# One predicated copy per score bank, a new switch table for the planner, and plain steps placed one by one

## The chip, the cores and the metric

The kernel runs on one core of one Trainium2 chip. The metric is the device time of one execution in microseconds (us); lower is better. Five engines work side by side, each on a queue of its own that it takes in order: TensorE (PE in the profile, with its weight loads listed apart as PEld), VectorE (DVE), ScalarE (ACT), GpSimd (POOL) and SyncE (SP, which starts the transfers). They wait for one another only through semaphores.

## The reference

```python
def _attn_ref(q, k, v):                      # q, k, v: (8, 8, 576, 64) float32
    scores = scale * np.matmul(q, k.transpose(0, 1, 3, 2))
    bias = slopes[:, None, None] * (-np.abs(rel))[None, :, :]
    mask = (rel >= 0) & (rel < 128)          # each row sees itself and the 127 before it
    scores = np.where(mask, scores + bias[None], -1e9)
    attn = softmax(scores)                   # max, exp, sum + 1e-9, divide
    return np.matmul(attn, v)

def _moe_ref(x, w_gate, w_val, w_out):       # x: (4608, 512), d_ff = 1536
    gate = sigmoid(x @ w_gate)
    return (gate * (x @ w_val)) @ w_out
```

The attention output, heads side by side, is the x of the gated feed-forward part.

## The kernel before

The attention is cut into 32 units, one for a batch and a pair of heads (576 rows of two heads, nine blocks of 128 rows). In a unit, `scores` works on four blocks at a time (a stage): TensorE writes the scores of 128 query rows against the keys that they can see into a bank of PSUM; a predicated copy on VectorE folds the two triangles that the window leaves into one square of 128 by 128; a custom VectorE instruction (line 394) adds the bias and takes the row minimum; ScalarE takes the exponential (397). For three blocks together, `probabilities` adds 1e-9 and inverts the sums on VectorE (412, 414), scales the rows (417 on ScalarE or 418 on VectorE, as the planner chooses), turns the three squares on TensorE (422), copies them out of PSUM (183 or 184) and masks them on GpSimd (433). When nine blocks are done, `values` multiplies with v (483), and copies and one addition (495) bring the result out; it is stored to DRAM as `xs`.

The first eight units ("whole") use matmuls of 64 by 128 for the scores and one copy of 128 partitions for a bank (line 386). The 24 units behind them ("fine") use the array as four squares of 64 by 64: `quarters` writes only the visible quarters, score matmuls are line 369, and the fold is two copies of 64 partitions for each bank (line 382), one for each half of the rows.

TensorE's other work during the attention is `gates1`, the gate and value products of four of the twelve chunks of d_ff for the first 3072 tokens: six tiles of 512 tokens, each with eight sums of twelve full-array matmuls of 512 columns (line 540, 576 in all). These are the plain steps. They take x of one tile at a time from a buffer `x1` that is used again for the next tile, through two banks. In the kernel before, `project` adds them to the plan in threes (one chunk of x in three products of high and low parts). Behind the last plain step come `gates2` (line 622) and `results` (line 731), with full-array matmuls alone.

Nothing of this order stands in the code as such. Every step is added to a `Graph` with an engine, an estimated cost, its reads and writes, and a wish time `want`. `order` then picks, again and again, the step that could start earliest by these costs (ties by `want`; plain steps have the latest), and `play` writes the instructions in order of the planned start. On the chip each engine keeps that order: a step that isn't ready holds everything behind it on its engine. The field `mode` says how TensorE's array is cut for a step; a step of another mode than the one ahead is put off by a fixed time:

```python
            if o.eng == "PE" and o.mode != mode:
                mode = o.mode
                o.start += SWITCH / 2
```

Until 30 us, `play` also fills TensorE's planned holes with dummy matmuls (line 243).

Of the kernel before, what the change touches and what calls it, by code (L numbers as in the profile page):

```python
# [12 lines left out]
ALU = mybir.AluOpType  # L13
PSUM = bass.MemoryType.PSUM

P = 128
B, H, S, D = 8, 8, 576, 64
# [24 lines left out]
RPACE = 6.5  # L42
SLACK = 0.5
W0, WSTEP = 25.0, 1.0
SWITCH = 0.2
WARM = 30.0
YIELD = {"DVE": 0.1, "POOL": 0.0}
NRAW = 2
# [11 lines left out]
class Graph:  # L60
# [38 lines left out]
    def order(self):  # L99
        free = dict.fromkeys(self.LAT, 0.0)  # L100
        free["PE"] = 1.5
        wait = []
        port = moved = 0.0
        mode = 0
        for o in self.ops:
            if not o.left:
                wait.append(o)
        n = 0
        while n < len(self.ops):
            best = None  # L110
            for o in wait:
                least = min(way[1] for way in o.ways)
                for k, way in enumerate(o.ways):
                    e, cost, lat, shared, emit = way
                    s = max(free[e], o.ready, port if shared else 0.0)
                    key = (s + cost - least + (YIELD[e] if k else 0.0), o.want, o.seq)
                    if best is None or key < best[0]:
                        best = key, o, way, s
            key, o, (o.eng, o.cost, o.lat, shared, o.emit), o.start = best
            if o.eng == "PE" and o.mode != mode:  # L120
                mode = o.mode
                o.start += SWITCH / 2
            if o.eng == "PE" and o.start < WARM:
                gap = (o.start - free["PE"] - 0.2) // (0.25 if free["PE"] > 5.0 else 0.45)
                if gap > 0:
                    self.fill.append((free["PE"] + 0.01, int(gap)))
            wait.remove(o)
            if o.size:
                moved = max(moved, o.start + 1.7) + o.size
                o.lat = moved + 0.4 - o.start  # L130
            free[o.eng] = o.start + o.cost
            if shared:
                port = o.start + o.cost
            n += 1
            for i in o.outs:
                d = self.ops[i]
                same = o.eng == "PE" and d.eng == "PE"
                d.ready = max(d.ready, o.start + (o.cost if same else o.lat + d.slack))
                d.left -= 1
                if not d.left:  # L140
                    wait.append(d)
        return sorted(self.ops, key=lambda o: (o.start, o.seq))
# [10 lines left out]
def dve_cost(n, psum=False, two=False):  # L153
    return 0.07 + n * (0.00104 if psum or two else 0.00053)
# [7 lines left out]
def attention_gated_ffn(ctx: ExitStack, tc: tile.TileContext, qd, kd, vd, wg, wv, wo, out):  # L162
    nc = tc.nc
    ctx.enter_context(tc.manual_schedule())
    g = Graph()
# [38 lines left out]
    rel = ring[:, 0:3 * P].rearrange("p (a q) -> p a q", a=3)  # L204
    nc.gpsimd.iota(rel[:, 0], [[-1, P]], base=0, channel_multiplier=1, allow_small_or_imprecise_dtypes=True)
    before = att.tile([P, 2, P], I32, name="before")
    swap = att.tile([P, 2, D], I32, name="swap")
# [15 lines left out]
    nc.vector.tensor_scalar_mul(r0[:, 4], r0[:, 1], 0.5)  # L223
    for p in range(1, NPAIR):
        nc.vector.tensor_scalar_mul(relm[p], r0, 4.0 ** -p)
    for a in range(2):
        nc.gpsimd.tensor_scalar(swap[0:D, a], rel[0:D, 0, 0:D], 0.0, None, op0=ALU.is_ge)
        nc.gpsimd.tensor_copy(swap[D:P, a], rel[D:P, 1, D:P])

    xs = [dram.tile([KC, P, S], F32, name=f"xs{b}") for b in range(B)]  # L230
    hs = [[dram.tile([NFC // 2, P, HALVES[b // 2]], F32, name=f"hs{k}_{b}") for b in range(2 * NT2)] for k in range(2)]
# [4 lines left out]
    mm = [ps_m.tile([P, NB], F32, name=f"mm{i}") for i in range(8)]  # L236
    sp = [t.rearrange("p (a q) -> p a q", a=2) for t in mm[2:6]]
    tp, avp, avo = mm[6].rearrange("p (a q) -> p a q", a=4), mm[7], mm[5]
    TP, TAIL, AVP, AVO = ("mm", 6), ("mm", 6, TRI), ("mm", 7), ("mm", 5)

    def warm(n):
# [12 lines left out]
    w1 = lambda kind, part_: T(moe, "w1", [P, 2, 2, FC1, DM], F32R, tag="wA")[:, "gv".index(kind), part_]  # L254
# [89 lines left out]
    def scores(blks):  # L344

        u0, i0 = blks[0]
        want = u0.when(i0)
        slack = 0.0 if u0.n < HEAD else SLACK
        spot = [(k % 2, k // 2) for k in range(len(blks))]
        fine = u0.n >= HEAD  # L350
# [20 lines left out]

        used = sorted({place(r, a) // 2 for r, a in spot}, key=lambda b: [place(r, a) // 2 for r, a in spot].index(b))
        of_bank = {b: [(u, i, place(r, a) % 2) for (u, i), (r, a) in zip(blks, spot) if place(r, a) // 2 == b] for b in used}
        cost = 0.163 * len(blks) + 0.1 if fine else sum(max(0.216 if i == 0 else 0.432 for u, i, a in on) for on in of_bank.values())
        g.add("PE", cost, quarters if fine else whole,
              [("qr", u.l, i) for u, i in blks] + [("kr", u.l, j) for u, i in blks for j in (i - 1, i) if j >= 0],
              [("mm", 2 + b) for b in used], want, slack=slack, release=max(u.rel(i) for u, i in blks), mode=1)
        for b in used:
            if fine:
                for h in range(2):  # L380
                    col, to, of = slice(h * D, h * D + D), D + h * D, 0 if h else 3 * D
                    g.add("DVE", dve_cost(2 * D, psum=True), lambda b=b, col=col, to=to, of=of: nc.vector.copy_predicated(  # L382
                        sp[b][col, :, to:to + D], swap[col], sp[b][col, :, of:of + D]), ["before"], [("mm", 2 + b)], want)
            elif a := [a for u, i, a in of_bank[b] if i]:
                a0, a1 = a[0], a[-1] + 1
                g.add("DVE", dve_cost((a1 - a0) * P, psum=True), lambda b=b, a0=a0, a1=a1: nc.vector.copy_predicated(  # L386
                    sp[b][:, a0:a1, P:], before[:, a0:a1], sp[b][:, a0:a1, 0:P]), ["before"], [("mm", 2 + b)], want)
# [18 lines left out]
    def probabilities(u, i0):  # L406
        m, _, st, pb, kst, kpb = three_of(u, i0)
        want = u.when(i0 + TRI)
        slack = 0.0 if u.n < HEAD else SLACK
        n, kb = TRI, ("both", m % NBOTH)  # L410
        both = lambda: T(att, f"both{m % NBOTH}", [P, TRI, P], F32)
        g.add("DVE", 0.07, lambda: nc.vector.tensor_scalar_add(st()[:, 6:9], st()[:, 3:6], 1.0e-9),
              [(kst, 3 + e) for e in range(n)], [(kst, 6)], want)
        g.add("DVE", 0.09, lambda: nc.vector.reciprocal(st()[:, 6:9], st()[:, 6:9]), [], [(kst, 6)], want)  # L414
        for e in range(n):
            args = lambda e=e: (pb()[:, e], pb()[:, e], st()[:, 6 + e:7 + e])
            g.add("ACT", 0.3, lambda args=args: nc.scalar.mul(*args()), [(kst, 6)], [(kpb, e)], want,  # L417
                  ways=[("DVE", 0.16, True, lambda args=args: nc.vector.tensor_scalar_mul(*args()))])  # L418

        def transpose():  # L420
            for e in range(n):
                nc.tensor.transpose(tp[:, e], pb()[:, e], ident)  # L422

        g.add("PE", 0.11 * n + 0.1, transpose, [(kpb, e) for e in range(n)], [TP], want, slack=slack)
        copy(lambda: both(), lambda: tp[:, 0:n], n * P, [TP], [kb], want, psum=True)
        for own in range(2):
            step, cmp, mult = ([1, P], ALU.is_ge, -1) if own else ([-1, P], ALU.is_gt, 1)

            def spread(own=own, step=step, cmp=cmp, mult=mult):
                f0 = 2 * i0 + own
                nc.gpsimd.affine_select(pt(u)[:, f0:f0 + 2 * n - 1:2, :], both(), [[0, n], step], cmp, 0.0,  # L433
                                        base=0, channel_multiplier=mult)

            g.add("POOL", 0.13 + 0.12 * n, spread, [kb], [("pt", u.n % NPT, i0 + e, own) for e in range(n)], want)
# [3 lines left out]
    def values(u):  # L440
        want = u.when(NBLK + 1)
        slack = 0.0 if u.n < HEAD else SLACK
        spots = ((0, NB, lambda: avp), (NB, S, lambda: tp[:, TRI, 0:S - NB]))
        runs = []
        for t0, t1, to in spots:
            todo = [[], []]
            for e in range(2):
                for c in range(NBLK):

                    a, b = max(c * P, e * S + t0), min((c + 2) * P, NBLK * P, e * S + t1)  # L450
# [11 lines left out]
        fine = u.n >= HEAD  # L462
# [12 lines left out]
        def quarters():  # L475
            seen = pt(u).rearrange("p s t -> p (s t)")
            begun = set()
            for _, e, jj, t0, t1 in quarter:
# [6 lines left out]
                begun.add((k, e))  # L485

        need = [("pt", u.n % NPT, i, own) for i in range(NBLK) for own in range(2)]
        g.add("PE", 1.5 if fine else 1.81 + 0.15, quarters if fine else matmuls, need + [("vr", u.l)],
              [AVP, TAIL] + [AVO] * fine, want, slack=slack, mode=1 if fine else 2)
        xt = lambda: T(att, f"xt{u.s}", [P, S], F32)  # L490
        for (t0, t1, to), key in zip(spots, (AVP, TAIL)):
            copy(lambda t0=t0, t1=t1: xt()[:, t0:t1], lambda t0=t0, t1=t1, to=to: to()[:, 0:t1 - t0], t1 - t0, [key], [("xt", u.s, t0)],
                 want, psum=True)
# [26 lines left out]
    def gates1(t0, n):  # L520
        F = FIRST
        xr = lambda: xrow()[:, :, 0:n]
        a = t0
        while t0 and a < t0 + n:
            b = a // S
            e = min((b + 1) * S, t0 + n)
# [3 lines left out]
            a = e  # L530
# [4 lines left out]
        def project(kind, i):  # L535
            s = bank()
            for c in range(KC):
                def three(c=c):
                    for k, (wi, x) in enumerate(((0, 0), (1, 0), (0, 1))):
                        nc.tensor.matmul(mm[s][:, 0:n], w1(kind, wi)[:, i, c * P:(c + 1) * P], x1(x)[:, c, 0:n],  # L540
                                         start=(k == 0 and c == 0), stop=(k == 2 and c == KC - 1))
                g.add("PE", 3 * (n / 2400 + 0.0177), three, [("w1", kind, wi, i) for wi in range(2)] + [("xhi", c), ("xlo", c)],
                      [("mm", s)], 1.0e6)
            return s

        for i0 in range(0, FC1, GRP):
            grp = range(i0, min(FC1, i0 + GRP))
            for i in grp:
                s = project("g", i)
# [384 lines left out]
```

## Time and profile before

| what | value |
|---|---|
| three runs | 1003.98, 1005.03, 1005.67 us; median 1005.03 |
| the profiled execution | 1005.5 us, of which the span of the profile is 1003.7 |
| mean granted TensorE clock | 0.996 |
| PE busy | 986.3 us (98%), 6498 instructions |
| DVE busy | 837.0 us (83%), 2104 instructions |
| ACT busy | 526.9 us (52%) |
| POOL busy | 123.6 us (12%) |
| first score matmul of the fine units | 59.05 us |
| last matmul of the attention | 320.57 us |
| last plain step, first matmul of line 622 | 335.6 us |

The busy share of PE is a weak sign, since matmuls overlap: a plain step shows about 410 ns, while they follow each other every 230 ns. The waits ahead of the weight loads (PEld) show more of what TensorE lacked. "Releaser" is the instruction whose semaphore ended a wait, and "issue" is time in which nothing that the profile shows was waited for.

### The profile page before, as it was taken

The page shows a single profiled execution, that of the slowest core. Times are in us where ns is not written, and L with a number is a line of the kernel's source. Part 1 is how long each engine was busy: PE and PEld are TensorE (multiplying, and loading weights), DVE is VectorE, ACT ScalarE, POOL GpSimd, SP SyncE. Part 2 cuts the span into 40 slices and gives each one's busy share as a digit, 9 for nine tenths or more (in the row PEclk, how much of TensorE's full clock was granted, in tenths as well). Part 3 has the DMA queues.
Part 4 walks back from the last instruction along what each step waited for, and adds up shares of the span by engine and source line. Part 5 has one row for each costly group of instructions (what it writes and reads, how often), then busy time and mean ns, then how long its engine had stood idle before and what let it go on. Part 6 is the DMA issues. An engine that isn't in the chain of part 4 may idle for free.

```text
span 1003.7 us, 18582 instructions
## 1 busy us (share of the span) xinstructions
PE 986.3 (98%) x6498; PEld 836.5 (83%) x6498; DVE 837.0 (83%) x2104; ACT 526.9 (52%) x1365; POOL 123.6 (12%) x225
## 2 busy tenths in 40 slices
PE   9899899999999999999999999999999999999998
PEld 8667677677777888788888999999998888889998
DVE  8998888988986999977943897599899988888883
ACT  6998887677875554534623454354356232312230
POOL 2333334123322001000000000000010000000000
PEclk9999899999999999999999999999999999999999
DMA  8765767564734454467421344144635635252601
GB/s 290 259 225 182 228 225 274 177 219 169 243 108 152 160 168 155 151 247 237 145 92 63 112 141 147 48 152 126 226 102 189 218 115 182 71 168 89 189 16 63
DMA packets 82845, 163.74 MB, mean 163 GB/s; under 512 B 8256, under 2 KB 34752, under 8 KB 82752
## 3 DMA queue, kind: packets, MB, share of 16 engines
q1 hardware_dynamic: 82752, 162.56, 48.6%
q8 instruction: 51, 0.84, 0.3%
q14 instruction: 42, 0.34, 0.1%
HBM read 112.20 MB, written 50.33 MB: 162 GB/s over the span
## 4 chain that ended last, share of the span: by engine, by line
PE 75%; DVE 18%; ACT 4%; issue 2%; DMA 1%; POOL 0%; SPq 0%; ACTq 0%; DVEq 0%; POOLq 0%
PE mm L622 34%; PE mm L731 26%; PE mm L540 7%; DVE mm L382 3%; PE mm L369 2%; DVE pb L394 2%; ACT pb L397 2%; PE mm L483 2%; DVE work L280 2%; PE mm L422 2%; DVE pb L418 1%; DVE x L192 1%; DVE ring L556 1%; DVE mm L386 1%; PE mm L243 1%
## 5 line engine op out<-in xcount | busy, mean ns | idle before, releaser
L540 PE MATMUL mm<-x,w 128*128 128x512 f32 x576 | 157.3, 409 | 1.7 <-DVE x L192 1.0
L622 PE MATMUL mm<-cxA,w2s 128*128 128x384 f32 (+1 forms) x684 | 145.0, 361 | 0.0
L622 PE MATMUL mm<-cxB,w2s 128*128 128x384 f32 (+1 forms) x684 | 143.9, 361 | 0.0
L397 ACT ACTIVATE pb<-pb,st 128x128 f32<-128x128 f32 x288 | 112.9, 395 | 44.6 <-DVE st L394 43.8
L622 PEld LDWEIGHTS mm<-cxA,w2s 128*128 128x128 f32 x684 | 123.8, 188 | 12.8
L622 PEld LDWEIGHTS mm<-cxB,w2s 128*128 128x128 f32 x684 | 123.6, 188 | 12.7
L433 POOL TENSOR_SCALAR_AFFINE_SELECT pt<-both 128x384 f32<-128x384 f32 x192 | 100.9, 549 | 203.2 <-ACT both L183 183.5
L540 PEld LDWEIGHTS mm<-x,w 128*128 128x128 f32 x576 | 101.1, 189 | 29.4 <-issue 7.6
L183 ACT COPY ring<-mm 128x512 f32<-128x512 f32 (+1 forms) x143 | 75.4, 534 | 78.4 <-PE mm L622 77.1
L731 PE MATMUL mm<-cxA,wos 128*128 128x512 f32 (+1 forms) x540 | 113.6, 368 | 0.0
L731 PE MATMUL mm<-cxB,wos 128*128 128x512 f32 (+1 forms) x540 | 113.3, 367 | 0.0
L731 PEld LDWEIGHTS mm<-cxB,wos 128*128 128x128 f32 x540 | 98.4, 188 | 12.6
L731 PEld LDWEIGHTS mm<-cxA,wos 128*128 128x128 f32 x540 | 98.4, 188 | 12.6
L633 ACT ACTIVATE sg<-mm 128x512 f32<-128x512 f32 (+1 forms) x96 | 52.2, 545 | 107.4 <-PE mm L622 59.8
L629 DVE TENSOR_TENSOR mm<-mm,ring 128x512 f32<-128x512 f32 (+1 forms) x96 | 60.2, 629 | 49.9 <-PE mm L622 49.6
L280 DVE SCALAR_TENSOR_TENSOR work<-work 128x512 int32<-128x512 int32 x104 | 70.9, 694 | 0.5
L394 DVE CUSTOM_DVE_ANT_0 pb<-mm,relm 128x128 f32<-128x128 f32 x288 | 68.6, 285 | 1.7
L191 POOL TENSOR_TENSOR work<-work 128x256 f32<-128x256 f32 x19 | 16.6, 878 | 399.7 <-ACT ring L183 210.1
L422 PE MATMUL mm<-ident,pb 128*128 128x128 f32 x288 | 52.7, 288 | 8.9 <-ACT both L183 4.5
L382 DVE COPY_PREDICATED mm<-swap,mm 64x128 f32<-64x128 int32 x216 | 56.1, 294 | 5.4 <-PE mm L369 1.6
L417 ACT ACTIVATE pb<-pb,st 128x128 f32<-128x128 f32 x163 | 56.3, 396 | 7.1 <-DVE st L414 6.5
L743 ACT ACTIVATE ring<-mm 128x512 f32<-128x512 f32 (+1 forms) x40 | 22.3, 556 | 69.5 <-PE mm L731 69.5
(110 smaller groups left out, 1594.1 us busy)
## 6 DMA issues: line engine op xcount, KB each, us to landing
hs<-ring SPq DMA_DIRECT2D x72, 256.0 KB, 2.1
kr<-in_k_dram SPq DMA_DIRECT2D x31, 576.0 KB, 5.0
work<-in_moe_w_gate_dram SPq DMA_DIRECT2D x20, 512.0 KB, 3.7
work<-in_moe_w_val_dram SPq DMA_DIRECT2D x20, 512.0 KB, 4.5
qr<-in_q_dram SPq DMA_DIRECT2D x31, 320.0 KB, 5.4
vr<-in_v_dram SPq DMA_DIRECT2D x32, 288.0 KB, 3.5
xs<-xt SPq DMA_DIRECT2D x32, 288.0 KB, 4.1
hs<-ring SPq DMA_DIRECT2D x48, 192.0 KB, 1.9
```

The costliest lines, as they stand in the source:

```text
L183: g.add("ACT", act_cost(n, psum), lambda: nc.scalar.copy(out(), src()), reads, writes, want, release=release, ways=[("DVE", dve_cost(n, ps ...
L280: g.add("DVE", dve_cost(DM, two=True), lambda word=word, scalar=scalar, o0=o0: nc.vector.scalar_tensor_tensor(bits(), wraw(s)[:, :, word], ...
L382: g.add("DVE", dve_cost(2 * D, psum=True), lambda b=b, col=col, to=to, of=of: nc.vector.copy_predicated(sp[b][col, :, to:to + D], swap[col ...
L394: g.add("DVE", 0.21, lambda: nc.vector.tensor_tensor_reduce(pb()[:, e], sp[j // 2][:, j % 2, first:first + P], relm[u.p][:, w], op0=ALU.ad ...
L397: g.add("ACT", 0.39, lambda: nc.scalar.activation(pb()[:, e], pb()[:, e], AF.Exp, bias=st()[:, e:e + 1], scale=-1.0, accum_out=st()[:, 3 + ...
L417: g.add("ACT", 0.3, lambda args=args: nc.scalar.mul(*args()), [(kst, 6)], [(kpb, e)], want, ways=[("DVE", 0.16, True, lambda args=args: nc ...
L422: nc.tensor.transpose(tp[:, e], pb()[:, e], ident)
L433: nc.gpsimd.affine_select(pt(u)[:, f0:f0 + 2 * n - 1:2, :], both(), [[0, n], step], cmp, 0.0, base=0, channel_multiplier=mult)
L540: nc.tensor.matmul(mm[s][:, 0:n], w1(kind, wi)[:, i, c * P:(c + 1) * P], x1(x)[:, c, 0:n], start=(k == 0 and c == 0), stop=(k == 2 and c = ...
L622: nc.tensor.matmul(mm[b][:, 0:N], w2t(i, wp)[:, wk, c * P:(c + 1) * P], combo(k, xp)[:, c, 0:N], start=(start and c == 0 and j == 0), stop ...
L629: g.add("DVE", dve_cost(N, psum=True), lambda: nc.vector.tensor_tensor(o(), bk(b)(), a(), op=ALU.add), [("mm", b), *reads] if okeys else r ...
L731: nc.tensor.matmul(mm[banks_[i]][:, 0:N], wot(e * HC + c, wp)[:, k, i * P:(i + 1) * P], hcombo(s, xp)[:, c, 0:N], start=(start and e == c ...
```

## The change

Four things are changed.

1. In the fine units one predicated copy of 128 partitions folds both halves of a bank. Its views have four dimensions: for each of two blocks the two inner squares of 64 are overwritten by squares 3 and 0. The mask `swap` is zero where nothing is to be copied, and its set-up on GpSimd is one memset and two instructions in place of four.
2. The fixed switch time gives way to a table, `TURN`, by the mode ahead and the mode behind; transposes get a mode of their own (3).
3. Planned costs of some steps are other numbers: scores, values, transposes, and the scaling of rows on VectorE (0.196 in place of 0.16).
4. `project` adds each plain step by itself, with the one weight part and the one x part that it reads.

```diff
-SWITCH = 0.2
+TURN = {(0, 1): 0.1, (0, 3): 0.0, (3, 1): 0.14, (3, 0): 0.085, (1, 0): 0.215, (1, 3): 0.14}
...
             if o.eng == "PE" and o.mode != mode:
+                o.start += TURN[mode, o.mode]
                 mode = o.mode
-                o.start += SWITCH / 2
...
-    for a in range(2):
-        nc.gpsimd.tensor_scalar(swap[0:D, a], rel[0:D, 0, 0:D], 0.0, None, op0=ALU.is_ge)
-        nc.gpsimd.tensor_copy(swap[D:P, a], rel[D:P, 1, D:P])
+    nc.gpsimd.memset(swap, 0)
+    nc.gpsimd.tensor_scalar(swap[0:D, 0], rel[0:D, 0, 0:D], 0.0, None, op0=ALU.is_ge)
+    nc.gpsimd.tensor_copy(swap[D:P, 1], rel[D:P, 1, D:P])
+    swaps = swap.unsqueeze(1).broadcast_to((P, 2, 2, D))
...
+    fold = [t.rearrange("p (a s q) -> p a s q", a=2, s=4) for t in mm[2:5]]
...
             if fine:
-                for h in range(2):
-                    col, to, of = slice(h * D, h * D + D), D + h * D, 0 if h else 3 * D
-                    g.add("DVE", dve_cost(2 * D, psum=True), lambda b=b, col=col, to=to, of=of: nc.vector.copy_predicated(
-                        sp[b][col, :, to:to + D], swap[col], sp[b][col, :, of:of + D]), ["before"], [("mm", 2 + b)], want)
+                g.add("DVE", dve_cost(4 * D, psum=True), lambda b=b: nc.vector.copy_predicated(
+                    fold[b][:, :, 1:3], swaps, fold[b][:, :, 3::-3]), ["before"], [("mm", 2 + b)], want)
...
             for c in range(KC):
-                def three(c=c):
-                    for k, (wi, x) in enumerate(((0, 0), (1, 0), (0, 1))):
+                for k, (wi, x) in enumerate(((0, 0), (1, 0), (0, 1))):
+                    def one(c=c, k=k, wi=wi, x=x):
                         nc.tensor.matmul(mm[s][:, 0:n], w1(kind, wi)[:, i, c * P:(c + 1) * P], x1(x)[:, c, 0:n],
                                          start=(k == 0 and c == 0), stop=(k == 2 and c == KC - 1))
-                g.add("PE", 3 * (n / 2400 + 0.0177), three, [("w1", kind, wi, i) for wi in range(2)] + [("xhi", c), ("xlo", c)],
-                      [("mm", s)], 1.0e6)
+                    g.add("PE", n / 2400 + 0.0177, one, [("w1", kind, wi, i), (("xhi", "xlo")[x], c)], [("mm", s)], 1.0e6)
```

How the change moves instructions shows at three places. Numbers behind a name are those of the buffer; a row with x3 stands for three like instructions in a row.

VectorE, a stage of a late fine unit, before: `mm3` and `mm4` are the two score banks of the stage, `xt0` the result of an earlier unit, `x1` the plain steps' input.

```order
L382 COPY_PREDICATED mm3_147<-swap_79,mm3_147 64x2x64
L495 TENSOR_TENSOR xt0_385<-mm5_149,xt0_385 128x512
L382 COPY_PREDICATED mm3_147<-swap_79,mm3_147 64x2x64
L382 COPY_PREDICATED mm4_148<-swap_79,mm4_148 64x2x64
L394 ISA pb2_223,st0_193<-mm3_147,relm2_86 128x128
L394 ISA st0_193 128x1
L382 COPY_PREDICATED mm4_148<-swap_79,mm4_148 64x2x64
L394 ISA pb3_267,st1_214<-mm3_147,relm2_86 128x128
```

The same stage now:

```order
L382 COPY_PREDICATED mm3_146<-swap_79,mm3_146 128x2x128
L382 COPY_PREDICATED mm4_147<-swap_79,mm4_147 128x2x128
L394 ISA pb2_222,st0_192<-mm3_146,relm2_86 128x128
L394 ISA st0_192 128x1
L394 ISA pb3_266,st1_213<-mm4_147,relm2_86 128x128
L394 ISA st1_213 128x1
L394 ISA pb3_266,st1_213<-mm3_146,relm2_86 128x128
```

Four copies of 64 partitions have become two of 128, and the bias instructions of the stage (394) follow at once.

TensorE, plain steps between two transposes of a late fine unit, before: `mm0` and `mm1` are the two banks of the plain steps, `pb0` and `pb1` hold probabilities that are transposed into `mm6`, and the last row is the first score matmul of the next stage.

```order
L422 MATMUL mm6_150<-ident_71,pb0_192 128x128 x3
L540 MATMUL mm1_145<-x1_412,w1_435 128x512 x6
L422 MATMUL mm6_150<-ident_71,pb1_213 128x128 x3
L540 MATMUL mm0_144<-x1_412,w1_435 128x512 x3
L369 MATMUL mm2_146<-kr0_152,qr0_154 64x192
```

Around the transpose of `pb1` now:

```order
L540 MATMUL mm0_143<-x1_413,w1_443 128x512 x3
L540 MATMUL mm1_144<-x1_413,w1_443 128x512 x3
L422 MATMUL mm6_149<-ident_71,pb1_212 128x128 x3
L540 MATMUL mm0_143<-x1_413,w1_443 128x512 x3
L540 MATMUL mm1_144<-x1_413,w1_443 128x512 x2
L540 MATMUL mm0_143<-x1_413,w1_443 128x512 x2
L540 MATMUL mm1_144<-x1_413,w1_443 128x512
L540 MATMUL mm0_143<-x1_413,w1_443 128x512
```

Runs of plain steps no longer come in multiples of three, and two sums can stand open in the two banks in turn.

TensorE, the end of the attention, before: the first row is the last matmul with v (`mm6`, four in a row), the last one the first of `gates2`.

```order
L483 MATMUL mm6_150<-pt1_345,vr1_172 64x64 x4
L540 MATMUL mm0_144<-x1_412,w1_435 128x512 x6
L540 MATMUL mm1_145<-x1_412,w1_435 128x512 x12
L540 MATMUL mm0_144<-x1_412,w1_435 128x512 x12
L540 MATMUL mm1_145<-x1_412,w1_435 128x512 x12
L540 MATMUL mm0_144<-x1_412,w1_435 128x512 x12
L540 MATMUL mm1_145<-x1_412,w1_435 128x512 x12
L622 MATMUL mm0_144<-cxA_4240,w2s4_2299 128x512 x6
```

The same place now, up to the middle of the plain steps:

```order
L483 MATMUL mm6_149<-pt1_345,vr1_171 64x64 x4
L540 MATMUL mm1_144<-x1_413,w1_443 128x512 x3
L540 MATMUL mm0_143<-x1_413,w1_443 128x512 x12
L540 MATMUL mm1_144<-x1_413,w1_443 128x512 x12
L540 MATMUL mm0_143<-x1_413,w1_443 128x512 x5
L540 MATMUL mm1_144<-x1_413,w1_443 128x512 x3
L540 MATMUL mm0_143<-x1_413,w1_443 128x512 x7
L540 MATMUL mm1_144<-x1_413,w1_443 128x512 x9
```

Behind these stand six more sums of twelve. So 66 plain steps stood behind the last step of the attention, and 123 stand there now; the sixth tile, whose 96 steps begin at the row with x5, was begun ahead of the last two units, and now begins after the last.

More of the change, by code (lines that the diff above doesn't have):

```diff
@@ L373, in scores @@
         of_bank = {b: [(u, i, place(r, a) % 2) for (u, i), (r, a) in zip(blks, spot) if place(r, a) // 2 == b] for b in used}
-        cost = 0.163 * len(blks) + 0.1 if fine else sum(max(0.216 if i == 0 else 0.432 for u, i, a in on) for on in of_bank.values())
+        cost = 0.163 * len(blks) + 0.05 if fine else sum(max(0.216 if i == 0 else 0.432 for u, i, a in on) for on in of_bank.values())
         g.add("PE", cost, quarters if fine else whole,
@@ L417, in probabilities @@
             g.add("ACT", 0.3, lambda args=args: nc.scalar.mul(*args()), [(kst, 6)], [(kpb, e)], want,
-                  ways=[("DVE", 0.16, True, lambda args=args: nc.vector.tensor_scalar_mul(*args()))])
+                  ways=[("DVE", 0.196, True, lambda args=args: nc.vector.tensor_scalar_mul(*args()))])
         def transpose():
@@ L422, in transpose @@
                 nc.tensor.transpose(tp[:, e], pb()[:, e], ident)
-        g.add("PE", 0.11 * n + 0.1, transpose, [(kpb, e) for e in range(n)], [TP], want, slack=slack)
+        g.add("PE", 0.1 * n, transpose, [(kpb, e) for e in range(n)], [TP], want, slack=slack, mode=3)
         copy(lambda: both(), lambda: tp[:, 0:n], n * P, [TP], [kb], want, psum=True)
@@ L487, in values @@
         need = [("pt", u.n % NPT, i, own) for i in range(NBLK) for own in range(2)]
-        g.add("PE", 1.5 if fine else 1.81 + 0.15, quarters if fine else matmuls, need + [("vr", u.l)],
-              [AVP, TAIL] + [AVO] * fine, want, slack=slack, mode=1 if fine else 2)
+        g.add("PE", 1.43 if fine else 1.86, quarters if fine else matmuls, need + [("vr", u.l)],
+              [AVP, TAIL] + [AVO] * fine, want, slack=slack, mode=1)
         xt = lambda: T(att, f"xt{u.s}", [P, S], F32)
```

## The prediction

> **What bounds the kernel now.** I read the stages first (busy time by window), then the chain of waits, then the waits of one engine, then single rows. By window, each row gives the stretch, its length, and the busy time of PE, PEld, DVE, ACT and POOL with their instructions, then the clock:
>
> ```profile
> span 1003.7 us, 18582 instructions
> 59.00:321.00 262.00, 252.96 (x2735) 189.19 (x2733) 223.31 (x1043) 201.54 (x735) 87.42 (x165) 0.99 0.60 199
> 321.00:336.00 15.00, 15.00 (x67) 12.41 (x67) 13.24 (x17) 4.75 (x7) 0.00 (x0) 1.00 0.21 79
> 336.00:1004.00 668.00, 663.67 (x3275) 592.42 (x3274) 546.42 (x765) 272.14 (x432) 16.49 (x18) 1.00 0.43 141
> ```
>
> From 336 us on TensorE works without a hole (663.7 of 668 us), and the change alters nothing in those steps. So it can only move the moment at which line 622 begins:
>
> ```profile
> 320.50 15.26 PE L540 MATMUL mm<-x,w 128*128 128x512 f32 x66
> 335.59 1.75 PE L622 MATMUL mm<-cxA,w2s 128*128 128x512 f32 x7
> ```
>
> The 66 plain steps take 335.59 - 320.50 = 15.1 us, 0.229 us each. All of them must be done by then, wherever they stand; moving one is worth something only if it fills a hole of TensorE. How large the holes are between 59 and 336 us shows in the waits of the weight loads (total us, times, longest), named by what ended them:
>
> ```profile
> PEld mm L369 <- issue: 8.8, 34, 0.4
> PEld mm L540 <- issue: 7.2, 26, 0.3
> PEld mm L483 <- issue: 4.7, 14, 0.4
> PEld mm L422 <- ACT both L183: 7.7, 15, 1.7
> PEld mm L369 <- DVE st L394: 5.7, 16, 1.1
> PEld mm L540 <- DVE x L192: 2.6, 4, 1.0
> PEld mm L422 <- DVE xt L184: 2.1, 2, 1.1
> PEld mm L422 <- ACT xt L183: 1.9, 2, 1.3
> PEld mm L483 <- POOL pt L433: 1.6, 5, 0.4
> PEld mm L422 <- ACT pb L417: 1.6, 6, 0.5
> PEld mm L422 <- ACT pb L397: 1.4, 4, 0.5
> ```
>
> The three "issue" rows, 20.7 us in 74 places (0.28 each), stand where the array changes between full and quarter use: nothing is waited for, so this is the price of a switch. The other eight, 24.6 us, are waits for attention data while plain steps stood behind them in the queue. That sum is about all that a better order can win. What makes the data late shows in the chain of waits of 59 to 345 us (286 us), grouped by line:
>
> ```profile
> by line: PE mm L540 25.2%; DVE mm L382 9.4%; PE mm L369 8.5%; PE mm L483 7.6%; PE mm L422 6.4%; ACT pb L397 6.1%; DVE pb L394 5.0%; issue 4.5%; DVE ring L556 2.8%; DVE work L280 2.8%; DVE x L192 2.6%; DVE xt L495 2.3%; DVE pb L418 2.1%; DVE
> ```
>
> The folding copies (382) are the second entry, 9.4% of 286 = 26.9 us. So the attention is limited by TensorE and VectorE in turn: VectorE is busy 223.3 of 262 us (85.2%).
>
> **The change part by part.** The rows for the VectorE and ScalarE steps (busy us, mean ns) are:
>
> ```profile
> L382 DVE COPY_PREDICATED mm<-swap,mm 64x128 f32<-64x128 int32 x216 | 56.1, 294 | 5.4 <-PE mm L369 1.6
> L386 DVE COPY_PREDICATED mm<-before,mm 128x256 f32<-128x256 int32 x28 | 11.4, 420 | 1.6 <-PE mm L359 1.5
> L418 DVE TENSOR_SCALAR pb<-pb,st 128x128 f32<-128x128 f32 x125 | 32.8, 301 | 1.2
> L417 ACT ACTIVATE pb<-pb,st 128x128 f32<-128x128 f32 x163 | 56.3, 396 | 7.1 <-DVE st L414 6.5
> L192 DVE TENSOR_TENSOR x<-xr,x 128x512 fp32r<-128x512 f32 x20 | 13.9, 707 | 0.2
> L556 DVE SCALAR_TENSOR_TENSOR ring<-sg,mm 128x512 f32<-128x512 f32 x24 | 16.4, 681 | 1.7 <-PE mm L540 1.6
> ```
>
> *Copies.* 108 banks cost 56.1 / 108 = 0.519 us each with two copies. The new copy isn't in the trace. It covers 128 partitions and 256 elements like line 386 of the first units, which takes 11.4 / 28 = 0.407. Its bounds are 0.26 (one old copy, half the elements) and 0.52 (two old copies, if the deeper view costs as much again). I take 0.407, since elements, partitions and memory are the same. That frees 108 x 0.112 = 12.1 us of VectorE; only the part on the chain shortens the span: 26.9 x (1 - 0.407 / 0.519) = 5.8 us. Bounds: 0 (price 0.52, or TensorE is late next everywhere) and 12.1 (the whole of it on the path). What is late next is the bias step (394, 5.0%) and the exponential (397, 6.1%).
>
> *Switches.* Counted over the whole order, changes between full-array steps (540, 422) and quarter steps (369, 483) go from 132 to 137: plain to quarter 38 to 45 and back 34 to 40, transpose to quarter 27 to 23 and back 33 to 29. Five more at 0.28 cost 1.4 us. Below, 0 (a transpose may switch at the same price as a plain step or more); above, 13 x 0.28 = 3.6, if those at transposes are free. The Trainium skill, "TensorEngine Tiling", section Key Properties, says that a change of the tiling mode drains TensorE. It names no price; by it each added switch is a loss that no order hides, which speaks against the change, and the "issue" rows agree with it at 0.28 us.
>
> *Plain steps one by one.* Their number and length stay. Two things move. Ahead of the first quarter score, 29 stand where 18 stood, so 11 x 0.229 = 2.5 us of plain work goes into the head. Its holes:
>
> ```profile
> 25.00:59.00 34.00, 31.06 (x247) 1.00 0.79 267
> PEld mm L422 <- ACT pb L417: 3.1, 8, 1.1
> PEld mm L422 <- ACT both L183: 2.0, 2, 1.1
> PEld mm L422 <- ACT xt L183: 1.2, 2, 0.8
> ```
>
> TensorE shows 34 - 31.1 = 2.9 us without any matmul there, and 6.3 us of waits at transposes. The holes cannot all lie where x is ready, so I take half, -1.2 us (bounds 0 and -2.5). At the end of the attention 123 plain steps remain in place of 66: 57 x 0.229 = 13.1 us of cover leave the attention. That wins nothing by itself; it is the place of a rival below. A waiting score or transpose still holds the plain steps behind it, as before, since the queue is in order.
>
> *Scaling rows.* 14 go from VectorE (32.8 / 125 = 0.262) to ScalarE (56.3 / 163 = 0.345): -3.7 us on one, +4.8 on the other, and five copies go the other way. ScalarE is busy 201.5 of 262 us (77%) and has the room; I take 0, with bounds -3.7 and +4.8.
>
> *Set-up of the mask.* Three GpSimd instructions in place of four, in the first microseconds, while the first fine score stands at 59 us: 0; without that cover, a few tenths.
>
> *Tail.* The sixth tile's plain steps now all stand behind the attention. Its x must be split before line 622's first input can be loaded into the same buffer. Before:
>
> ```profile
> 312.32 0.69 DVE x L192
> 313.07 1.48 SPq L188 DMA_DIRECT2D xr<-xs x3
> 320.66 0.22 DVE L184 COPY xt<-mm 128x64 f32<-128x64 f32 x1 [6.33 <-PE mm L483]
> 322.80 1.22 DVE L665 TENSOR_TENSOR xr<-xr 128x1024 f32<-128x1024 f32 x1
> 326.72 2.36 DVE L192 TENSOR_TENSOR cxA<-xr,cxA 128x1024 fp32r<-128x1024 f32 x2
> ```
>
> From the last x to the first two parts of cxA it took 329.1 - 313.0 = 16.1 us, 6.3 of them with VectorE idle. Now there are 96 x 0.229 = 22 us less some 2 us for the first split, so 20: enough. I take 0 (bound: 3 us late, if VectorE's weight work, which now fills the idle 6.3 us, runs over).
>
> Sum: -5.8 + 1.4 - 1.2 = -5.6 us. The profiled execution took 1005.5 us (span 1003.7), 0.5 above the median of 1005.03; so 999.9 for it, and 999.5 for the median.
>
> **The rivals.** *Slower: the thinner cover.* The place is every score and transpose of the fine units. By the sum, the stretch 59 to 321 shrinks from 262 to 262 - 13.1 - 2.5 + 1.4 - 5.8 = 242.0 us. VectorE has 223.3 - 12.1 - 4 x 0.7 (x of the sixth tile) - 2.4 x 0.68 (line 556 of 57 steps) = 206.8 us to do in it, 85.5%, where it now does 85.2%. If it holds only 82%, the stretch takes 252.2 us, TensorE waits 10.2 us more, and the time is 1009.7. It decides at 206.8 / 247.6 = 83.5%: below that, the change loses. For it: the eight waits above show that TensorE meets late data already. Against: the copies' 12.1 us come out of just this stretch.
>
> *No change.* The deeper view makes the new copy cost 0.52, or what VectorE gains is lost at line 397. Then +1.4 - 1.2, 1005.2. For it: no row has this view. Against: line 386 has strided views too.
>
> *Faster: the clock isn't cut.* Each row is a stretch with PE's busy time and the granted clock:
>
> ```profile
> 108.00:110.00 2.00, 0.86 (x21) 0.51 (x20) 1.53 (x7) 2.00 (x10) 0.49 (x2) 1.00 0.72 194
> 110.00:112.00 2.00, 1.07 (x9) 0.55 (x9) 1.91 (x12) 0.91 (x5) 0.99 (x2) 0.90 0.86 298
> 107.00:119.00 12.00, 9.44 (x108) 0.72 0.50 152
> ```
>
> With no plain steps at hand (the second tile isn't split), TensorE is half idle from 108 to 112 us, and the clock falls; 12 x (1 - 0.72) = 3.4 us are lost. The new order starves at the same place, over two units as before, so the sum keeps the loss. If shorter copies keep TensorE busy enough there, 3.4 us more are won: 996.1. A second such hole would cost 3.4. The Trainium skill, "TensorE: Matmul & The Clock Gate", section What's actually happening, says that the clock halves after an idle window of about 3.4 us, and comes back after as long a busy one; by that rule the cut should vanish here if the hole shrinks at all, while the row shows a cut after a hole that was only half empty.
>
> **How the numbers follow.** The forecast (996.5 to 1003.0) has 0.48; deeper gains (clock kept, or more of the copies on the path) 0.18; no change 0.20; the thinner cover 0.14. About 0.2%, 2 us, is what a measurement of this kernel tells from none, so faster (below 1003.0) has 0.48 + 0.18 = 0.66, same 0.20, slower (above 1007.0) 0.14. The low end is copies wholly on the path and the clock kept: 1005.0 - 12.1 - 3.4 + 1.4 = 990.9. The high end, 1007.0, leaves out the slower rival.
>
> **What would show it.** Right: 108 copies of about 0.41 us; their share of the chain near 7.5%; line 622 beginning near 330 us; the eight waits near 19 us; the same 665 us behind. Wrong: copies of 0.5 us or more; VectorE under 83.5% busy in the stretch of the fine units with longer waits at 369 and 422; line 622 beginning after a hole of TensorE; a second cut of the clock.

## The result and the profile after

The changed kernel takes 994.49 us (median of 4 runs, 994.12 to 995.47) against 1004.92 us before (4 runs): 10.4 us less, ratio 0.9898 with a 95% interval of 0.9881 to 0.9915. The forecast was 999.5, a range of 990.9 to 1007.0, and faster at 0.66. The sign and the range hold; the size is nearly twice the forecast's 5.6, and the experiments show that its main term, the copies, was far too small.

The same stretches of the profiled execution as before (PE, PEld, DVE, ACT and POOL busy, then the clock):

```profile
span 993.6 us, 18500 instructions
59.00:321.00 262.00, 258.10 (x2816) 197.47 (x2817) 218.51 (x962) 208.07 (x757) 89.48 (x166) 1.00 0.63 210
336.00:993.00 657.00, 652.02 (x3224) 582.91 (x3222) 530.68 (x736) 261.76 (x417) 17.38 (x18) 1.00 0.42 138
```

TensorE's start of `gates2` (now line 621) and the plain steps ahead of it:

```profile
293.78 1.65 PE L483 MATMUL mm<-pt,vr 64*64 64x192 f32 x40
295.36 28.40 PE L540 MATMUL mm<-x,w 128*128 128x512 f32 x123
323.60 4.66 PE L621 MATMUL mm<-cxA,w2s 128*128 128x512 f32 x18
```

The attention ends at 295.4 us (320.6 before), 123 plain steps follow without a hole, and `gates2` begins at 323.60 in place of 335.59: 12.0 us earlier. Of these, 1.9 are lost behind it: 993.6 - 323.6 = 670.0 us, where it was 1003.7 - 335.6 = 668.1.

The chain of waits of 59 to 345 us, by line, and the largest waits of the weight loads from 59 to 336 us:

```profile
by line: PE mm L540 43.5%; PE mm L371 14.7%; PE mm L483 12.3%; PE mm L422 10.5%; PE mm L621 6.4%; PE mm L459 2.1%; issue 1.5%; DMA work<-in_moe_w_gate_dram 1.4%; ACT pb L397 1.3%; ACT both L183 0.9%; ACT pb L417 0.9%; DVE work L282 0.5%; DV
PEld mm L371 <- issue: 12.1, 46, 0.4
PEld mm L540 <- issue: 7.6, 27, 0.3
PEld mm L483 <- issue: 5.1, 16, 0.4
PEld mm L422 <- ACT both L183: 3.7, 5, 0.9
PEld mm L540 <- DVE x L192: 2.0, 5, 0.7
PEld mm L422 <- ACT pb L397: 1.1, 4, 0.3
```

VectorE has nearly left the chain: the folds, 9.4% of it before, come behind the entries shown, so they have 0.5% at most, and TensorE's own lines make up nearly all. The wait of scores for the bias step (5.7 us before) is 0.5, below the rows shown. All waits for data in this stretch sum to 14.2 us; before it was 28.0. The switches rose: 24.8 us in 89 places in the three "issue" rows, for 20.7 in 74.

The folding copies and the scaling of rows:

```profile
L382 DVE COPY_PREDICATED mm<-swap,mm 128x256 f32<-128x256 int32 x108 | 41.5, 421 | 5.4 <-PE mm L371 4.8
L418 DVE TENSOR_SCALAR pb<-pb,st 128x128 f32<-128x128 f32 x111 | 28.0, 291 | 0.8
L417 ACT ACTIVATE pb<-pb,st 128x128 f32<-128x128 f32 x177 | 60.6, 395 | 6.8 <-DVE st L414 5.9
```

A merged copy costs 41.5 / 108 = 0.384 us of VectorE; the forecast took 0.407, the two old ones took 0.519.

### The profile page after: what moved, and what is told of

Same layout as the page of the kernel before. It is cut to its first block, busy times and chain, and to the rows that moved or that the text cites. A ratio compares the mean times of both kernels' runs of the same rounds, so it can differ in the third digit from the quotient of the medians.

```text
span 993.6 us, 18500 instructions
## 1 busy us (share of the span) xinstructions
PE 978.5 (98%) x6502; PEld 833.7 (84%) x6502; DVE 813.8 (82%) x1987; ACT 527.3 (53%) x1374; POOL 128.0 (13%) x224
## 4 chain that ended last, share of the span: by engine, by line
PE 91%; ACT 3%; DVE 3%; issue 1%; DMA 1%; POOL 0%; ACTq 0%; POOLq 0%; SPq 0%
PE mm L621 37%; PE mm L730 26%; PE mm L540 13%; PE mm L371 4%; PE mm L422 4%; PE mm L483 4%; PE mm L361 1%; ACT pb L397 1%; PE mm L245 1%; PE mm L459 1%; ACT pb L417 1%; ACT both L183 1%; DMA hs<-ring 1%; DVE work L282 0%; DMA work<-in_moe_w_gate_dram 0%
## 5 line engine op out<-in xcount | busy, mean ns | idle before, releaser
L540 PE MATMUL mm<-x,w 128*128 128x512 f32 x576 | 160.1, 410 | 1.3 <-ACT sg L549 0.5
L621 PEld LDWEIGHTS mm<-cxB,w2s 128*128 128x128 f32 x684 | 123.5, 188 | 12.8 <-ACT ring L183 0.2
L433 POOL TENSOR_SCALAR_AFFINE_SELECT pt<-both 128x384 f32<-128x384 f32 x192 | 102.9, 559 | 183.3 <-ACT both L183 139.6
L397 ACT ACTIVATE pb<-pb,st 128x128 f32<-128x128 f32 x288 | 112.5, 394 | 11.8 <-DVE st L394 11.4
L417 ACT ACTIVATE pb<-pb,st 128x128 f32<-128x128 f32 x177 | 60.6, 395 | 6.8 <-DVE st L414 5.9
L397 ACT ACTIVATION_READ_ACCUMULATOR pb<-pb,st 128x1 f32 x288 | 54.8, 190 | 0.0
```

The lines of the kernel that those rows point to most:

```text
L397: g.add("ACT", 0.39, lambda: nc.scalar.activation(pb()[:, e], pb()[:, e], AF.Exp, bias=st()[:, e:e + 1], scale=-1.0, accum_out=st()[:, 3 + ...
L621: nc.tensor.matmul(mm[b][:, 0:N], w2t(i, wp)[:, wk, c * P:(c + 1) * P], combo(k, xp)[:, c, 0:N], start=(start and c == 0 and j == 0), stop ...
```

## The experiments

Twelve kernels were timed, each in five rounds against the kernel before. M is the merged copy, T the switch table with the new costs, S the single plain steps.

| run | what | us | ratio, 95% interval |
|---|---|---|---|
| e1 | M | 992.19 | 0.9878 [0.9865, 0.9892] |
| e2 | T | 1000.90 | 0.9966 [0.9954, 0.9979] |
| e3 | S | 1003.34 | 0.9986 [0.9977, 0.9995] |
| e4 | order of before, merged copy | 991.32 | 0.9867 [0.9853, 0.9880] |
| e5 | before, clock kept by dummies | 1003.86 | 0.9990 [0.9981, 0.9998] |
| e6 | order of after, two copies | 1022.73 | 1.0179 [1.0165, 1.0193] |
| e7 | M and T | 991.22 | 0.9863 [0.9847, 0.9879] |
| e8 | M and S | 989.91 | 0.9852 [0.9838, 0.9865] |
| e9 | after, old scaling cost | 987.44 | 0.9821 [0.9808, 0.9835] |
| e10 | M and S, new scaling cost | 988.09 | 0.9831 [0.9818, 0.9845] |
| e11 | after, slack 0.55 | 996.70 | 0.9920 [0.9907, 0.9932] |
| e12 | M and S, slack 0.55 | 989.21 | 0.9838 [0.9825, 0.9852] |

**One part at a time.** e1, e2 and e3 make one of the three edits to the kernel before, word for word as in the diff above (e1 the copies and the mask; e2 the table, modes and costs; e3 `one` in place of `three`).

> Only the folding copies are merged (two planned steps become one); switch time, costs and triples are those of before. Theory A (the fold's time on VectorE is what shortens the attention; the two other edits are worth about nothing): 994 to 999 us, 60% or more of the change's 10.4 us. Theory B (what counts is where the plan puts the plain steps, by the new table and the single steps): 1002 to 1005 us, though VectorE is 14 us less busy. In either case about 108 copies of 0.38 to 0.42 us.

> Only the switch table, the transposes' own mode and the planned costs are the new ones; two copies for a bank and triples stay. Theory A: 1003 to 1007 us, no change. Theory B: 998 to 1002 us.

> Only the plain steps are placed one by one; two copies, old switch time and costs. Theory A: 1003 to 1007 us (the number of switches, 140 before and 141 here, moves nothing). Theory B: 998 to 1002 us, with the waits of the weight loads for attention data down from 28 us by 3 or more.

The merged copy alone gives 12.8 us, more than the whole change. The table gives 4.1 by itself and the single steps 1.6. Theory A has the direction in e1, but 992.19 lies 1.8 us below its range: the copies are worth even more than it said. e2 lies in theory B's range, so theory A is wrong that the table is worth nothing by itself. e3 lies in theory A's range, and theory B's sign is missing there: the waits for data from 59 to 336 us are 25.9 us for 28.0, down by 2.1 and not by 3.

The granted clock differs between executions of one kernel, and in e2 the time goes with it: five executions at 1.0 took 1000.04 to 1001.17 us, three at 0.996 or 0.997 took 1003.54 to 1003.88. In e3 three at 1.0 took 1002.60 to 1003.45, eight at 0.996 or 0.997 took 1002.75 to 1004.99. So part of the 4.1 us of the table depends on where the clock is cut, and how often.

**The shorter fold with nothing moved.** In e4 the plan is that of before, and so is each engine's order; two folds are planned for a bank, and only the second issues a copy.

```diff
                 for h in range(2):
-                    g.add("DVE", dve_cost(2 * D, psum=True), lambda b=b, col=col, to=to, of=of: nc.vector.copy_predicated(
-                        sp[b][col, :, to:to + D], swap[col], sp[b][col, :, of:of + D]), ["before"], [("mm", 2 + b)], want)
+                    g.add("DVE", dve_cost(2 * D, psum=True), lambda b=b, h=h: h and nc.vector.copy_predicated(
+                        fold[b][:, :, 1:3], swaps, fold[b][:, :, 3::-3]), ["before"], [("mm", 2 + b)], want)
```

> The order of before on every engine, kept by planning two folds for a bank and issuing one merged copy at the second one's place. It shows what a shorter fold is worth with nothing moved. Theory A: 997 to 1001 us, 4 to 8 us less than before, as the forecast's term of 5.8 has it. Theory B: 1002 to 1005, since each engine keeps an order that was made for the slower fold, and plain steps stand where they stood.

It takes 991.32 us, 13.7 less than before and 3.2 less than the changed kernel. In its profile the folds and the start of `gates2` (here line 623) read:

```profile
L383 DVE COPY_PREDICATED mm<-swap,mm 128x256 f32<-128x256 int32 x108 | 41.5, 419 | 1.4 <-PE mm L371 1.3
317.75 3.11 PE L541 MATMUL mm<-x,w 128*128 128x512 f32 x13
320.69 2.66 PE L623 MATMUL mm<-cxA,w2s 128*128 128x512 f32 x11
```

VectorE is relieved of 56.1 - 41.5 = 14.6 us, and `gates2` begins 335.59 - 320.69 = 14.9 us earlier: one for one, where both theories had less. The clock isn't cut from 107 to 119 us in this profile (1.00, where it was 0.72), and e5 below puts that at about 1 us of the 13.7. Theory A's kind is right, its size (4 to 8) is not; theory B is out. All waits for data from 59 to 336 us sum to 14.0 us, where it was 28.0; their fall is about the gain. The largest waits for data, with those of the first row 7.7 before, the scores for the bias step 5.7 before:

```profile
PEld mm L423 <- ACT both L183: 4.6, 8, 1.7
PEld mm L371 <- DVE st L395: 1.5, 5, 0.6
```

**The clock.** e5 adds six dummy matmuls to the kernel before, in the hole where the clock was cut.

```diff
         def quarters():
+            if turn == 30:          # the thirteenth fine stage
+                warm(2)
             for k in range(0, len(blks), 2):
                 ...
+            if turn == 29:          # the twelfth
+                warm(4)
```

> The kernel before, with six dummy matmuls (four behind the twelfth fine stage's scores, two ahead of the thirteenth's) in the hole of TensorE at 108 to 112 us, where the clock is cut; nothing else moves. Theory C (the cut costs its 3.4 us, and every variant that keeps the clock has them, merged copy or not): 1001 to 1002.5 us. Theory D (VectorE limits that stretch, so a slow TensorE costs little there): 1003.5 to 1005.5 us with the clock at 1.0. If the clock is cut all the same, 1005.

```profile
107.00:119.00 12.00, 11.00 (x130) 8.19 (x131) 10.90 (x51) 10.57 (x40) 5.09 (x10) 1.00 0.67 197
```

The clock stays at 1.00, and the time is 1003.86: 1.0 us less (0.2 to 1.9 by the interval), inside theory D's range and outside theory C's. VectorE is busy 10.9 of the 12 us, which fits theory D's reason, that VectorE limits this stretch and hides most of a slow TensorE.

This price need not hold elsewhere. In e7 (below, M and T) two executions at a clock of 1.0 took 989.56 and 989.66 us, and two at 0.996 took 992.78 and 992.91, 3.2 us more. The profile of one of the latter has its cut among the whole units:

```profile
45.00:55.00 10.00, 7.77 (x48) 5.53 (x45) 7.25 (x35) 8.35 (x35) 4.09 (x8) 0.66 0.58 190
```

There 10 x (1 - 0.66) = 3.4 us of clock were lost, and nearly all of it shows in the time.

**The new order with two copies.** e6 keeps the changed kernel's order and issues two copies where it has one.

```diff
+                def halves(b=b):
+                    for h in range(2):
+                        col, to, of = slice(h * D, h * D + D), D + h * D, 0 if h else 3 * D
+                        nc.vector.copy_predicated(sp[b][col, :, to:to + D], swap[col, h].unsqueeze(1).broadcast_to((D, 2, D)), sp[b][col, :, of:of + D])
+
-                g.add("DVE", dve_cost(4 * D, psum=True), lambda b=b: nc.vector.copy_predicated(
-                    fold[b][:, :, 1:3], swaps, fold[b][:, :, 3::-3]), ["before"], [("mm", 2 + b)], want)
+                g.add("DVE", dve_cost(4 * D, psum=True), halves, ["before"], [("mm", 2 + b)], want)
```

> The changed kernel's order on every engine, but each merged copy is issued as two of 64 partitions. Theory A' (the fold's time on VectorE is worth 10 to 14 us under any order): 1004 to 1009 us. Theory B (the new order is what brings the gain): 995 to 999 us.

```profile
L385 DVE COPY_PREDICATED mm<-swap,mm 64x128 f32<-64x128 int32 x216 | 64.0, 296 | 9.3 <-PE mm L371 2.4
PEld mm L371 <- DVE st L398: 10.0, 23, 0.9
PEld mm L426 <- ACT both L183: 7.3, 13, 1.3
PEld mm L544 <- DVE x L192: 5.0, 6, 1.5
349.46 1.75 PE L625 MATMUL mm<-cxA,w2s 128*128 128x512 f32 x7
```

1022.73 us: 28.2 more than the changed kernel, and 17.8 more than before. The pair costs more here than before (64.0 / 108 = 0.593 us; the two copies of a bank follow each other directly and their records don't overlap), so the run adds 22.5 us of VectorE, not 14.6. Even so it is over one for one. This is the course of the forecast's slower rival: 123 plain steps are kept for the end, VectorE can't hold the pace, and TensorE waits (10.0 us for the bias step alone) while plain work stands behind. How much of the loss is the thinner cover and how much the dearer copies, no run separates; that the order suits only the copy that it was made for is a reading of this one run. Theory A' has the direction and is short; theory B falls.

**Two parts at a time.**

> Merged copies and the new table with its costs; plain steps in threes. If the single steps are what the changed kernel loses against the merged copy alone (992.2): 990 to 993 us. If it is the table: 994 to 996.

> Merged copies and single plain steps; the old switch time and costs. If the single steps are what the changed kernel loses: 994 to 996 us. If it is the table: 990 to 993.

Both beat the changed kernel (991.22 and 989.91; e7's two executions at the lower clock do too, with 992.8), so neither the single steps nor the table is by itself what costs it 2.3 us against M alone. As they were written, the first expectation points to the single steps and the second to the table (989.91 is 0.1 below that range), so they contradict each other; the loss comes with the combination.

**Which number of the table.** The edits are one number each: in e9 the changed kernel's `("DVE", 0.196, ...)` goes back to 0.16; e10 puts 0.196 into M and S; e11 and e12 set `SLACK = 0.55` in the changed kernel and in M and S.

> The changed kernel with one planned cost put back: scaling of rows on VectorE 0.16 in place of 0.196. If the 14 scalings that this cost moves to ScalarE are what the changed kernel loses against merged copies with single steps (989.9): 989 to 992 us. If it is the switch table: 993 to 996.

> Merged copies and single steps with the old switch time and costs, but the new scaling cost of 0.196. If that cost is what loses: 993 to 996 us. If it is the switch table: 989 to 992.

> The changed kernel with a number that means nothing physical moved a little: the planner's slack 0.55 in place of 0.50. Same work, another order. Theory E (the 2 to 4 us between the variants with merged copies are accidents of the order): it lands anywhere in 989 to 997 us, at least 1 us from 994.5. If the table itself costs time: 994 to 995.5.

> Merged copies and single steps, old switch time and costs, slack 0.55 in place of 0.50. Theory E: anywhere in 987 to 994 us, at least 1 us from 989.9. If this combination is better for a reason of its own: 989 to 991.

With the old scaling cost the new table gives 987.44 us, the fastest of all and 7 us under the changed kernel. But the same cost does no harm under the old table (988.09 against 989.91). Both times lie below both of their ranges, so neither expectation holds as it was written. The two slack runs move by 2.2 us (e11, as theory E asked) and by 0.7 (e12, less than the 1 us that it asked for), so the time is reproducible to about that when a number without meaning is moved; the 7 us are beyond it, in one pair. Where they lie can be read in part. The first two rows are of the changed kernel, the last two of e9:

```profile
PEld mm L621 <- DVE ring L628: 3.3, 4, 2.0
402.64 1.66 PE L621 MATMUL mm<-cxC,w 128*128 128x512 f32 x6 [1.60 <-DVE ring L628]
PEld mm L621 <- DVE ring L628: 0.4, 1, 0.4
317.97 2.20 PE L621 MATMUL mm<-cxA,w2s 128*128 128x512 f32 x9
```

`gates2` begins 5.6 us earlier (317.97, last row), and the wait of 1.6 us behind it is gone. In the changed kernel that wait is for an addition on VectorE (line 628) that stands behind a step of 3.17 us, while GpSimd has a step of its own:

```profile
397.91 2.40 POOL L191 TENSOR_TENSOR cxB<-xr,cxB 128x1024 fp32r<-128x1024 f32 x1 [18.50 <-ACT cxB L183]
398.22 3.17 DVE L664 TENSOR_TENSOR xr<-xr 128x1024 f32<-128x1024 f32 x1
401.91 0.68 DVE L628 TENSOR_TENSOR ring<-mm,ring 128x512 f32<-128x512 f32 x1
404.24 1.21 DVE L664 TENSOR_TENSOR xr<-xr 128x1024 f32<-128x1024 f32 x1
```

The same step takes 1.21 us a little later. GpSimd has its step only in the changed kernel, e6 and e11, which share the table, the single steps and the cost of 0.196; in each of the three, VectorE's step beside it takes 3.17 us. From `gates2` to the end these three take 670.0 to 670.5 us, all the others 667.5 to 669.0. That GpSimd's step is what slowed VectorE's is likely, but wasn't tested. Ahead of `gates2`, TensorE is busy 32.08 of the 34 us from 25 to 59 us in e9, and 29.95 in the changed kernel. Why 0.196 and the new table together make the worse order stays open: no run takes that apart. e9 beats both kernels, with ratio 0.9821 against before.

## Why the prediction was right, and where its size failed

*What bounds the kernel.* Right: only the start of line 622 moved to any extent, the waits for data were what an edit could win, and VectorE made them. Of 28.0 us of such waits, 13.8 went.

*The copies' term: the step that failed.* The price was near (0.384 for 0.407), so VectorE was freed of 14.6 us for 12.1. The failing step is "only the part on the chain shortens the span", 26.9 us of the 56.1, hence 5.8 us. With nothing else moved the same relief gave 13.7 us in time (e4, about 1 us of it perhaps the clock). The chain follows, at each instant, the one releaser that came last; where it ran through a plain step, it counted TensorE. But the plain steps are a fixed amount of work that must be done anyway, so a stretch where the chain shows them need be no stretch where VectorE has room: the attention can be late there too and use up the cover. This reason is argued; what e4 and e6 show is the price. The forecast had named 12.1 us as the far bound, the whole on the path; that bound was near the truth. What would have told: VectorE at 85% busy, the largest of its own waits (12.5 us) for the exponential, and 28 us of waits at TensorE, nearly all for data on a way that runs through VectorE.

*Switches, +1.4.* The count (five more) was right for the order, and the price of 0.28 held (24.8 / 89 = 0.28). But 15 more places show, 4.1 us and not 1.4. Some may have fallen together with a late operand before and been booked as a wait for data; no run shows it. e2 and e3 show that the two order edits are worth 4.1 and 1.6 us alone; on top of the merged copy they are worth -2.3 (994.49 against 992.19). The forecast's 0.2 for both had no sight of the interaction.

*The head, -1.2.* Wrong. The first matmul with v of the fine units came at 98.43 us with 86 plain steps ahead of it, for 98.16 us and 87 before. The head has a hole of its own now, and the clock is cut there:

```profile
25.00:59.00 34.00, 29.95 (x221) 20.84 (x217) 30.33 (x162) 30.78 (x125) 11.34 (x20) 0.95 0.67 234
45.00:55.00 10.00, 7.76 (x61) 5.66 (x59) 7.86 (x37) 8.56 (x35) 4.31 (x8) 0.83 0.50 169
46.85 0.65 PE L422 MATMUL mm<-ident,pb 128*128 128x128 f32 x3 [1.59 <-ACT xt L183]
```

Before, TensorE was 9.30 of 10 us busy from 45 to 55 us; the plain steps that were moved in stand ahead of and behind this place, not in it.

*Scaling rows, 0.* The count was right (111 and 177). e9 shows that the cost behind it was not neutral: 987.44 with the old number in the changed kernel, though under the old table (e10) it does no harm.

*The tail, 0.* Right at the place that was asked: `gates2` begins without a hole. The 1.9 us lost behind it (mostly the wait of TensorE for VectorE's line 628, which ends at 402.6 us) weren't foreseen. "The same 665 us behind" was misread to begin with: by the rows of the kernel before it was 668.1, and it is 670.0 now.

*The rivals.* The thinner cover: e6 takes its course, and in the changed kernel it didn't strike, since the shorter fold came with it. No change: out, the deeper view costs nothing that shows (0.384 for 0.407). The clock:

```profile
108.00:110.00 2.00, 1.72 (x28) 1.00 0.83 253
110.00:112.00 2.00, 1.30 (x18) 1.00 0.93 262
```

In the profiled execution it isn't cut any more at 108 to 112 us, as that rival said, but a cut came in the head instead (0.95 over the 34 us from 25 to 59, 1.7 us of clock). The rival's price of 3.4 us was 1.0 at the old place (e5), while a cut in the head of e7 cost 3.2; no run isolates the one of the changed kernel.

*The signs.* The copies (0.384 us for "about 0.41") are as forecast. The others went further than forecast: the folds have at most 0.5% of the chain for 7.5%, `gates2` begins at 323.60 us for 330, and the eight waits sum to 8.1 us for 19.

*Luck.* That 994.49 lies well inside the range owes something to luck. The copies alone, in e4, gave 7.9 us more than their term, and came within 0.4 us of the range's low end; all the rest of the change together then cost 3.2 us, where the forecast had 0.2.

## What to carry to other kernels

When two engines feed each other and one of them has filler work that must be done in any case, a chain of waits can understate the other one (26.9 of 56.1 us here, where the whole counted): count the waits for its data and its idle time in the stretch as well. Test a faster step first with the order held fixed; here that alone gave 13.7 us, and the order that was planned for it gave 3.2 of them back. A plan that moves filler out of a stretch can be tied to the step times that it was made for (28.2 us lost when two copies gave VectorE 22.5 us more to do), and orders made from nearly the same numbers differ by up to 7 us, so several are worth timing.

## What the runs showed of the hardware

The predicated copy in PSUM costs 0.384 us for 128 partitions by 256 elements and 0.519 for two of 64 by 128 in the order of the kernel before, but 0.593 in e6, where the two of one bank always stand next to each other; why was not tried, and e6 also reads its mask through another view.

The clock's cut doesn't follow the busy share alone, and one kernel has it in some executions and not in others (e2, e3, e7 and e11). In the profiles it came in the kernel before after 0.86 and 1.07 of 2 us busy, and in the changed one in a stretch, 45 to 55 us, that was 7.76 of 10 us busy. It didn't come in e11, whose same stretch was as busy (first row), and not in e3 with less work than before at the old place (second row: 8.74 of 12 us; before, 9.44):

```profile
45.00:55.00 10.00, 7.77 (x70) 1.00 0.62 200
107.00:119.00 12.00, 8.74 (x116) 5.81 (x107) 10.85 (x49) 10.37 (x39) 4.73 (x11) 1.00 0.68 202
```

What a cut costs depends on its place: 1.0 us of 3.4 us of lost clock from 107 to 119 us (e5), 3.2 of 3.4 in the head (e7).
